# Attention pieces regrouped inside a dense FFN stream, with all queues in written order

## The chip, the cores and the metric

One core of one Trainium2 chip. The metric is the device time of one execution in microseconds (us), the median of several executions. "Span" is the time from the first to the last instruction in a profile; it is about 1.8 us shorter than the time of the same execution.

## The reference, cut to what matters

```python
# attention with K and V projected from 1024 rows to 64, then an FFN with a squared ReLU
k_proj = einsum('ks,bhsd->bhkd', E, k)        # q, k, v: 8 batches, 8 heads, 1024 rows, 64 columns
v_proj = einsum('ks,bhsd->bhkd', F, v)
attn   = softmax(q @ k_proj.T / 8)            # 1024 x 64 for each head
x      = (attn @ v_proj), heads side by side  # 8192 x 512
h      = maximum(x @ w_in, 0)                 # 512 -> 2048
out    = (h * h) @ w_out                      # 2048 -> 512
```

## The kernel before

The FFN of a batch is 62 steps in the order of TensorE's program. In batches 1 to 7 steps 0 to 15 and 31 to 46 are `x @ w_in` for half a batch (four matmuls of 512 columns each), and steps 16 to 30 and 47 to 61 are the second product, done as seven smaller products (in Strassen's manner) of 256-column matmuls. The attention of the next batch is cut into pieces, and tables say ahead of which step each goes:

```python
PIECES = {
    0: "transpose_q", 1: "copy_kp", 2: "copy_vp", 4: "copy_v_down",
    24: "scores 0, scores 1, exponentials 0", 25: "exponentials 1",
    27: "sums 0, values 0 0, reciprocals 0", 30: "values 0 1", 31: "normalize 0 0", 32: "normalize 0 1",
    47: "scores 2, scores 3, exponentials 2", 48: "exponentials 3",
    50: "sums 1, values 1 0, reciprocals 1", 53: "values 1 1", 54: "normalize 1 0", 55: "normalize 1 1",
}
```

A set of sums or values is eight matmuls side by side, each on 64 rows by 32 columns of TensorE's array (the eight start within 0.03 us). Their results go to a PSUM buffer (PSUM is the memory that TensorE writes to):

```python
def quads(self, g, weights):
    ps = att_psum([P, 2, TCH], F32)          # one of two PSUM buffers
    for a in range(2):
        for j in range(4):
            o, bank = PLACE[j % 2, a]
            nc.tensor.matmul(
                ps[32 * j:32 * j + 32, a, :], lhsT=weights(o, 4 * g + j),
                rhs=self.exp[2 * g + j // 2][o, bank, :], start=True, stop=True,
                tile_position=(o.start, 32 * j))
```

Q and the projected K are transposed by DMAs on SyncE's queue; Q, K and V are loaded, with a cast to bf16, by GpSimd's. There is one buffer each for Q, K, V and the transposed Q. The loop that places it all:

```python
with tc.manual_schedule(engines=ORDERED):    # TensorE, VectorE, ScalarE in written order
    ...
    for b in range(B):
        for n, g in enumerate(ffn_groups(b, cur.xT)):
            ...
            if nxt:
                for name, args in calls((BATCH_1, BATCH_2, PIECES)[min(b, 2)], n):
                    getattr(nxt, name)(*args)
                if n == (35, 12, 1)[min(b, 2)]:
                    ahead = load_batch(b + 2)
                if b and n == 53 and ahead:
                    ahead.project()
            g()
```

The softmax here doesn't subtract the row's maximum and nothing guards it: scores larger than these inputs give would overflow.

## Time and profile before

| | before |
|---|---|
| time, median | 487.8 us |
| span of the profile | 485.8 us |
| first FFN matmul | 19.90 us |
| batch 1 begins | 83.48 us |
| batch 1 / batches 2 to 5 / batch 6 / batch 7 | 60.26 / 57.61 / 55.89 / 55.8 us |

TensorE is busy 97% of the span, so the profile must be read for two small things: how long a batch is between the first FFN matmuls of two batches, and where a start comes later than the one before it explains. I call **cost in the stream** of a piece: the start of the first FFN matmul after it, less the start of the last one before it, less what that one takes alone (0.216 us with 512 columns, 0.109 with 256). The lines that carry the reading are in the prediction.

### The profile page before, as it was taken

The numbers are of one execution on the slowest core, as the hardware profiler recorded it, in microseconds if no ns is written. First come the engines' busy times: TensorE is split into PE (matmuls) and PEld (weight loads), VectorE is DVE, ScalarE is ACT, GpSimd is POOL, SyncE is SP. The second block draws the span as 40 slices with busy tenths as digits, with TensorE's granted clock in tenths as the row PEclk, the third lists the DMA queues.
The fourth block names the chain that finished last, engine by engine and source line by source line (L and its number), as shares of the span: only waits on it lengthen the run. The fifth ranks groups of instructions, "written<-read, shape, count | busy, mean of one in ns | idle before, by whom it ended". The sixth has DMA issues, their size and how long they took to land.

```text
span 485.8 us, 8378 instructions
## 1 busy us (share of the span) xinstructions
PE 472.6 (97%) x3614; PEld 292.3 (60%) x3614; DVE 315.4 (65%) x380; ACT 262.4 (54%) x414; POOL 33.2 (7%) x46
## 2 busy tenths in 40 slices
PE   4899999999999999999999999999999999999997
PEld 2444677475574845757475665747557474666656
DVE  2478855566848568495765848566694856848383
ACT  2487445665727556355655467264672746645351
POOL 6330020010020000100010000200000000000000
PEclk9999999999999999999999999999999999999999
DMA  9999999997389124991149921893232102020202
GB/s 162 204 205 206 164 144 219 235 170 178 46 145 226 30 88 86 172 187 44 44 89 194 162 88 20 141 220 66 88 74 68 45 0 88 2 88 0 88 0 88
DMA packets 72501, 55.46 MB, mean 114 GB/s; under 512 B 33936, under 2 KB 64656, under 8 KB 72464
## 3 DMA queue, kind: packets, MB, share of 16 engines
q0 software_dynamic: 30336, 29.36, 38.5%
q1 hardware_dynamic: 42128, 25.56, 20.7%
q8 instruction: 28, 0.46, 0.4%
q14 instruction: 9, 0.07, 0.0%
HBM read 59.24 MB, written 16.78 MB: 156 GB/s over the span
## 4 chain that ended last, share of the span: by engine, by line
PE 85%; DMA 10%; ACT 2%; POOL 1%; issue 1%; DVE 0%; POOLq 0%; DVEq 0%
PE ps_h L441 39%; PE ps_y L461 23%; PE ps_z L461 11%; DMA V_sb<-in_v_dram 7%; PE ps_x L461 5%; DMA w_in<-in_moe_w_in_dram 2%; PE ps_att L216 2%; PE ps_kv L175 2%; PE ps_att L201 2%; DMA kT<-kp 1%; ACT h_relu L492 1%; PE ps_kv L176 0%; POOL K_sb L91 0%; DVE hsq L500 0%; ACT hsq L498 0%
## 5 line engine op out<-in xcount | busy, mean ns | idle before, releaser
L441 PE MATMUL ps_h<-xT,w_in 128*128 128x512 bf16 x1024 | 225.0, 379 | 0.2 <-DMA w_in<-in_moe_w_in_dram 0.2
L500 DVE TENSOR_TENSOR hsq<-h_relu 128x1024 bf16<-128x1024 f32 x123 | 150.2, 1222 | 67.4 <-ACT h_relu L492 66.8
L492 ACT ACTIVATE h_relu<-ps_h 128x512 f32<-128x512 f32 x256 | 150.6, 597 | 66.2 <-PE ps_h L441 65.7
L441 PEld LDWEIGHTS <-w_in 128*128 128x128 bf16 x1024 | 99.5, 98 | 118.2 <-issue 1.8
L461 PEld LDWEIGHTS <-s 128*128 128x128 bf16 x1024 | 98.4, 98 | 19.6 <-issue 8.1
L461 PEld LDWEIGHTS <-hsq 128*128 128x128 bf16 x768 | 73.2, 98 | 19.4 <-issue 3.0
L461 PE MATMUL ps_y<-T,s 128*128 128x256 bf16 x512 | 62.4, 273 | 0.1
L574 DVE TENSOR_TENSOR o_sb<-ps_z,p_b 128x512 f32<-128x512 f32 x16 | 11.1, 692 | 52.9 <-issue 25.7
L455 DVE TENSOR_TENSOR s<-hsq 128x1024 bf16<-128x1024 bf16 x64 | 43.6, 684 | 0.0
L570 ACT COPY o_sb<-ps_y 128x512 f32<-128x512 f32 x15 | 8.8, 585 | 55.4 <-PE ps_y L461 55.4
L235 DVE TENSOR_TENSOR xT<-ps_att,rs 128x1024 bf16<-128x1024 f32 x28 | 33.0, 1217 | 7.3 <-ACT rs L229 7.3
L461 PE MATMUL ps_y<-w_out,hsq 128*128 128x256 bf16 x256 | 34.5, 273 | 0.3 <-DVE hsq L500 0.3
L461 PE MATMUL ps_x<-w_out,hsq 128*128 128x256 bf16 x256 | 33.2, 273 | 0.0
L461 PE MATMUL ps_y<-T,hsq 128*128 128x256 bf16 x256 | 31.7, 272 | 0.0
L208 ACT ACTIVATE expT<-ps_att 128x1024 bf16<-128x1024 f32 x28 | 27.4, 1028 | 6.4 <-PE ps_att L201 6.4
L461 PE MATMUL ps_z<-T,s 128*128 128x256 bf16 x256 | 30.8, 273 | 0.0
L461 PE MATMUL ps_z<-w_out,s 128*128 128x256 bf16 x256 | 30.6, 273 | 0.0
L570 ACT COPY p_b<-ps_y 128x512 f32<-128x512 f32 (+1 forms) x17 | 9.5, 560 | 28.1 <-PE ps_y L461 28.0
L78 POOL DMA_DIRECT2D Q_sb<-in_q_dram x7 | 6.1, 876 | 263.2 <-DMA qT<-Q_sb 262.8
L574 DVE TENSOR_TENSOR o_sb<-ps_y,p_d 128x512 f32<-128x512 f32 (+1 forms) x17 | 11.2, 660 | 19.2 <-PE ps_y L461 19.2
L228 ACT ACTIVATE rs<-ps_att 128x1024 f32<-128x1024 f32 x14 | 14.3, 1023 | 14.6 <-PE ps_att L216 14.6
L455 DVE TENSOR_TENSOR s<-s,hsq 128x1024 bf16<-128x1024 bf16 x32 | 21.9, 687 | 0.5
(74 smaller groups left out, 239.3 us busy)
## 6 DMA issues: line engine op xcount, KB each, us to landing
out_dram<-o_sb SPq DMA_DIRECT2D x30, 512.0 KB, 3.3
K_sb<-in_k_dram POOLq DMA_DIRECT2D x7, 1024.0 KB, 17.3
V_sb<-in_v_dram POOLq DMA_DIRECT2D x7, 1024.0 KB, 22.4
Q_sb<-in_q_dram POOLq DMA_DIRECT2D x7, 1024.0 KB, 9.6
w_in<-in_moe_w_in_dram POOLq DMA_DIRECT2D x8, 256.0 KB, 13.7
w_out<-in_moe_w_out_dram POOLq DMA_DIRECT2D x4, 512.0 KB, 13.2
K_sb<-in_k_dram POOLq DMA_DIRECT2D x2, 512.0 KB, 7.8
V_sb<-in_v_dram POOLq DMA_DIRECT2D x2, 512.0 KB, 12.7
```

What stands on the lines that cost most here:

```text
L175: nc.tensor.matmul(ps[0:KP, :], lhsT=ET[:, i, :], rhs=kv[:, :, i, :], start=f, stop=l)
L201: nc.tensor.matmul(ps[o, bank, :], lhsT=self.kT[r, 2 * pr + j, :], start=True, stop=True, rhs=self.qT[r, NT * (2 * pr + j):NT * (2 * pr + ...
L208: nc.scalar.activation(e[:], self.ps["s", pr][:], AF.Exp, scale=SCALE)
L228: nc.scalar.activation(rs[:], self.ps["r", g][:], AF.Ln)
L235: nc.vector.tensor_tensor(out=self.xT[:, 2 * g + e].rearrange("p a n t -> p a (n t)"), in0=self.ps["v", g, e][:], in1=self.rs[g][:], op=AL ...
L441: nc.tensor.matmul(ps[:], lhsT=w_in_blk(cb, fb), rhs=xT[:, cb, :, 2 * ch:2 * ch + 2], start=(cb == 0), stop=(cb == NCB - 1),)
L455: nc.vector.tensor_tensor(out=s[o][:, js], in0=x, in1=y, op=op)
L461: nc.tensor.matmul(ps[tb] if len(ps) == 2 else ps[0][:, tb], lhsT=lhs[:, j, tb * P:(tb + 1) * P], rhs=rhs[:, j], start=first and n == 0 an ...
L492: nc.scalar.activation(r[:, n], ps[:], AF.Relu)
L500: multiply = lambda: nc.vector.tensor_tensor(out=o, in0=r[:], in1=r[:], op=ALU.mult)
L570: nc.scalar.copy(to[:, t], ps)
L574: nc.vector.tensor_tensor(out=to[:, t], in0=ps, in1=more[:, t], op=ALU.add)
```

## The change

Its intent: fewer changes between FFN and attention on TensorE (five pieces a batch), pieces in batches 0 and 1 moved to where their data are there, and SyncE and GpSimd no longer ordered by the scheduler at build time but as written.

```diff
-ORDERED = {PE, DVE, Activation}
+ORDERED = {PE, DVE, Activation, Pool, SP}
     PIECES = {
-        0: "transpose_q", 1: "copy_kp", ...
-        24: "scores 0, scores 1, exponentials 0", 25: "exponentials 1",
-        27: "sums 0, values 0 0, reciprocals 0", 30: "values 0 1", ...
-        47: "scores 2, scores 3, exponentials 2", 48: "exponentials 3",
-        50: "sums 1, values 1 0, reciprocals 1", 53: "values 1 1", ...
+        1: "copy_kp", ...
+        20: "scores 0, scores 1, exponentials 0", 21: "exponentials 1",
+        23: "sums 0, values 0 0, reciprocals 0", 26: "normalize 0 0",
+        28: "scores 2, scores 3, exponentials 2", 29: "exponentials 3",
+        47: "values 0 1, sums 1, reciprocals 1", 48: "normalize 0 1",
+        53: "values 1 0, values 1 1", 54: "normalize 1 0", 55: "normalize 1 1",
     }
     BATCH_1 = {                                  # attention of batch 1, during batch 0
-        32: "project", 33: "copy_kp, transpose_q, copy_vp", ...
-        46: "scores 0, scores 1, ...", 49: "sums 0, values 0 0, ...", 52: "..., values 0 1", ...
-        54: "scores 2, scores 3, ...", 57: "sums 1, values 1 0, ...", 60: "values 1 1, normalize 1 1",
+        33: "project", 34: "copy_kp, transpose_q, copy_vp", ...
+        48: "scores 0, scores 1, ...", 51: "scores 2, scores 3, ...",
+        55: "sums 0, sums 1, logs 0, logs 1, inverses 0", 57: "inverses 1",
+        58: "values 0 0, values 0 1, ...", 61: "values 1 0, values 1 1, normalize 1 0",
     }
-    BATCH_2 = {**PIECES, ..., 9: "project", 10: "copy_kp", ...}
+    BATCH_2 = {12: "project", 13: "copy_kp, transpose_q", ..., 24: "scores 0, scores 1, ...",
+        27: "scores 2, scores 3, ...", 30: "sums 0, sums 1, logs 0", ...,
+        47: "values 0 0, values 0 1", 53: "values 1 0, values 1 1", ...}
     SECOND_HALF = {                              # second half of batch 0's own attention
-        9: "second_half 1 0, second_half 0 1",
+        9: "second_half 1 0", 10: "second_half 0 1",
-    ON_SCALAR = {(0, 1): (2, 4, 6), (1, 0): (4, 6)}
+    ON_SCALAR = {(0, 1): (2, 4, 6), (1, 0): (3, 5)}
-            elif b == 0:
+            elif b + ch == 1:                    # batch 1 too opens with x blocks 0 and 1 alone
+                    if b and n == 33 and ahead:
+                        ahead.transpose_q()
```

Cut: the split of the reciprocals into logs and inverses, one more square held back on VectorE in batch 0, three sums put off by two steps, the load order K, V, Q for batch 1, the start of batch 3's loads, and the last normalization of batch 1 after batch 0's last step.

## The prediction

> **What bounds the kernel now.** I read the page's engine row first, then the windows by batch, then what TensorE waited for, then the order of its work around the small attention matmuls, and last the queue of SyncE.
>
> The engine row of the page: TensorE (PE) is busy for nearly the whole span, VectorE and ScalarE are near two thirds.
>
> ```profile
> PE 472.6 (97%) x3614; PEld 292.3 (60%) x3614; DVE 315.4 (65%) x380; ACT 262.4 (54%) x414; POOL 33.2 (7%) x46
> ```
>
> The windows cut the span at the first FFN matmul of each batch (columns: stretch, length, then busy time of each engine). Start-up is the first 26 us, batch 0 ends at 83.48, batch 1 at 143.74.
>
> ```profile
> core 0: us, PE busy (x) PEld busy (x) DVE busy (x) ACT busy (x) POOL busy (x), PEclk, DMA share, GB/s
> 26.00:83.48 57.48, 56.19 (x488) 34.61 (x487) 41.08 (x55) 34.56 (x53) 6.74 (x8) 1.00 1.11 187
> 83.48:143.74 60.26, 60.00 (x450) 36.56 (x448) 38.37 (x46) 33.61 (x52) 5.26 (x6) 1.00 0.87 155
> 143.74:201.35 57.61, 57.61 (x435) 35.57 (x433) 38.81 (x45) 31.94 (x50) 2.63 (x3) 1.00 0.59 115
> 374.17:430.06 55.89, 55.81 (x419) 34.79 (x417) 37.93 (x43) 31.94 (x50) 0.00 (x0) 1.00 0.12 41
> ```
>
> Batches 2 to 5 take 57.61 us with TensorE busy in all of it. Batch 1 is longer mainly because two projections (of batches 2 and 3) fall into it; one takes 1.85 us (133.95 to 135.80 in the order of time). Only batches 0 and 1 have idle gaps. The list of TensorE's waits is short, and its first line belongs to the start, which the change leaves alone:
>
> ```profile
> PE ps_E L138 <- DVE e_bf L134: 5.6, 1, 5.6
> PE ps_att L201 <- DMA kT<-kp: 0.5, 1, 0.5
> PE ps_att L286 <- DMA Q_sb<-in_q_dram: 0.4, 1, 0.4
> PE ps_y L461 <- DVE hsq L500: 0.3, 1, 0.3
> PE ps_kv L176 <- DMA V_sb<-in_v_dram: 0.2, 1, 0.2
> ```
>
> The order of time in a settled batch shows what an attention piece costs inside the FFN stream (start, duration, what; only starts are used):
>
> ```profile
> 166.08 1.04 PE L461 MATMUL ps_y<-T,s 128*128 128x256 bf16 x8
> 167.04 0.41 PE L216 MATMUL ps_att<-expT,ones 64*32 64x512 bf16 x8
> 167.27 0.40 PE L216 MATMUL ps_att<-expT,vp 64*32 64x512 bf16 x8
> 167.60 1.05 PE L461 MATMUL ps_y<-T,s 128*128 128x256 bf16 x8
> 168.48 1.04 PE L461 MATMUL ps_x<-w_out,hsq 128*128 128x256 bf16 x8
> 169.43 1.03 PE L461 MATMUL ps_y<-T,hsq 128*128 128x256 bf16 x8
> 170.39 0.41 PE L216 MATMUL ps_att<-expT,vp 64*32 64x512 bf16 x8
> 170.74 1.05 PE L461 MATMUL ps_y<-T,hsq 128*128 128x256 bf16 x8
> ```
>
> Eight FFN matmuls run start to start in 0.88 us undisturbed (167.60 to 168.48), but in 0.96 us when a piece follows (166.08 to 167.04, 169.43 to 170.39). A piece of one set of eight costs 0.35 + 0.09 = 0.44 us, a piece of two sets 0.56 + 0.09 = 0.65 us. Two single sets joined into one piece so save 2 x 0.44 - 0.65 = 0.23 us.
>
> SyncE's queue around the second and third batch (start, time to issue):
>
> ```profile
> 57.73 5.02 SPq L167 DMA_TRANSPOSE qT<-Q_sb  x1
> 62.81 1.25 SPq L185 DMA_TRANSPOSE kT<-kp  x1
> 66.36 0.43 SPq L625 DMA_DIRECT2D out_dram<-o_sb  x1
> 79.29 12.77 SPq L167 DMA_TRANSPOSE qT<-Q_sb  x1
> 94.48 1.22 SPq L185 DMA_TRANSPOSE kT<-kp  x1
> ```
>
> The transpose of Q at 79.29 meets the loads of batch 2's K and V and takes 12.77 us to issue; the settled ones take 4.7.
>
> **What the Trainium skill says.** "TensorE: Matmul & The Clock Gate", section "Back-to-back issue gap", gives N/2.4 + 2.5 ns between matmuls on a warm clock: 216 ns for 512 columns, 109 for 256. The trace agrees: in the chain of work 64 FFN matmuls of 512 columns take 13.81 us (216 ns), 16 of 256 columns 1.75 us (109 ns), at a granted clock of 1.00. So what is left to gain is in the pieces and the waits, not in the FFN. "TensorEngine Tiling (Array Packing)", section "Key Properties", says that changing the tiling mode drains TensorE; the 0.09 us ahead of every piece, where 128x128 changes to 64x32, fits. "DMA: Bandwidth & Descriptors", section "Issuing engines are not separate DMA queues", says that DMAs of all issuing engines end on the same 16 and interleave; the 12.77 against 4.7 us above agrees. The same trace's transposes of Q land 6.7 us after issue at best, 7.3 in the median, 16.4 at worst.
>
> **The change part by part.** One FFN batch has 62 steps: 16 of four 512-column matmuls (0.863 us each) and 15 of mostly eight 256-column ones (0.873 us) for each half; in batch 0 both halves' first products come first.
>
> Fewer pieces. In PIECES, the third batch's table and the second's, six pieces a batch (scores, sums with values, values, twice) become five (scores, scores and three of two sets each). No matmul is added or removed. 7 batches x 0.23 = 1.6 us, all on TensorE's path, as TensorE has no slack.
>
> First half-batch. The transposes of Q's second half move one step later (9 to 10). They waited 0.40 us for Q, whose load landed at 29.7; a step is 0.86 us, so the 0.40 goes. A square is held back behind the copy of the transposes; VectorE has gaps there (0.8 and 1.3 us), so no cost.
>
> Second batch. Its projection moves from step 32 to 33. It started at 52.03 and its V landed at 52.63; it ended at 54.49, 2.46 us for 1.9. One step later, V is there: 0.56 saved. The transpose of K is now ahead of that of Q in SyncE's queue. K's copies end near 56, Q's load lands at 57.64, so Q is issued about as before and lands near 66.3, as before. The scores came at step 46 and waited until 66.72. They now come two steps (1.75 us) later, near 67.3, and the 0.5 us wait goes.
>
> Opening of batch 1. The last two x blocks come late by design: values 1 0 and 1 1 at step 61 and the last normalization after it, while the FFN opens with eight matmuls on blocks 0 and 1 (1.73 us). ScalarE: the four reciprocal activations (1.02 to 1.06 each) start at step 55 behind a copy, so the first reciprocal is ready 3.8 us after that step begins and the first normalization ends near 5.1. VectorE then does normalization (1.2), two adds (0.65 each) and the last two normalizations in a row. By this count values 1 1 waits some 0.2 us for its PSUM buffer (two, freed by the normalizations), and block 3 is ready 0.4 us before it is wanted. Cost +0.2.
>
> Third batch. The projection moves from step 9 to 12; V(2) landed at 91.48 and step 12 is near 92.4, so no wait. Q's transpose moves behind K's at step 13, after the loads. From the start of batch 1: 12 steps 10.4, projection 1.9 = 12.3; VectorE first finishes a sum that waits for ScalarE's square, then K's two copies, 13.9; K's issue 1.25, so Q is issued at 15.1 and lands 6.7 to 7.3 later: 21.8 to 22.4. The scores at step 24 come at 13.8 + 1.9 + 6.1 = 21.8. Cost 0 to 0.6, say +0.3. The 0.3 us wait for the last square in batch 1 should go with the squares moved to ScalarE at 3 and 5 and three sums put off: -0.26.
>
> Settled batches. Q's transpose moves to step 33 of the batch before; K's stays, now behind the last store, about 1.5 us later. K's landing took 10.5 us in the median, so near 12.5 after the batch's start; scores at step 20 come at 16.4. No wait, no gain.
>
> Sum: -1.6 - 0.40 - 0.56 - 0.5 - 0.26 + 0.2 + 0.3 = -2.8. From 487.81: 485.0 us.
>
> **Rivals.** First, a wait moves instead of going: Q(2)'s transpose lands late. If it met loads it would take 16.4 us and TensorE would lose about 9 us, 494. Against it: the loads of batch 3 stand behind Q's buffer, which is freed only when this transpose lands (GpSimd's waits on it total 262.8 us), so it runs nearly alone. A loss of 1 us is possible, giving 486.
>
> Second, given order blocks SyncE or GpSimd: a store waiting for VectorE holds a transpose behind it. SyncE waits 238 us in total for such adds, so blocking is real, but each transpose behind a store has slack of 4 us or more in the settled batches. If K landed 2 us after it is wanted in four batches, 493. GpSimd's order was already the written one at the start, so nothing is lost there.
>
> Third, the opening of batch 1 stalls by 1 to 2 us because the normalizations pile up: 486 to 487.
>
> Fourth, the waits go but what they hid appears behind them, so that only the pieces count: 486.2.
>
> **Range and chances.** The gains are small and mostly arithmetic of the pieces; the losses have the longer tail, so the range is 484.0 to 487.0 around 485.0. Faster by 2% needs 478.1: that is 6.9 us more than I find, and TensorE has no idle time to give it after the start: 0.01. Slower needs 497.6, several rivals at once: 0.015. Within 2%: 0.975.
>
> **What would show it.** Right: batches 2 to 5 near 57.4 us with five pieces; batch 0 shorter by about 1.5; no TensorE wait for Q's load, for V at the second projection, for K's transpose. Wrong: a TensorE wait for a transpose at batch 1's scores above 0.6 us; a wait for VectorE's x at 82 to 86 us; settled batches at 57.6, which would mean that joined pieces save nothing; waits of TensorE that repeat in every batch, which would mean that the queue order bites.

## The result, and the profile after

The changed kernel took 485.42 us in the median of four executions (483.81 to 485.61), the kernel before 487.83 beside it. The ratio is 0.9938, 95% interval 0.9911 to 0.9965. The median lies in the prediction's range, 485.0 in 484.0 to 487.0.

The profiled execution was the fastest of the four, 483.81 us, with a span of 482.0. The engine row of the page after, and of TensorE's six waits the longest and the last two of the list:

```profile
PE 470.4 (98%) x3614; PEld 293.1 (61%) x3614; DVE 313.2 (65%) x380; ACT 261.8 (54%) x414; POOL 33.2 (7%) x46
```

```profile
PE ps_E L141 <- DVE e_bf L137: 5.6, 1, 5.6
...
PE ps_h L459 <- DVE xT L350: 0.4, 1, 0.4
PE ps_att L319 <- ACT expT L313: 0.2, 1, 0.2
```

All of these lie before 20.1 us. The waits for Q's load, for V, for K's transpose and for VectorE's square are gone. The windows by batch (same columns as in the prediction; batch 0 from 26 us, batch 1, batch 2, batch 6):

```profile
26.00:81.56 55.56, 55.44 (x490) 34.89 (x488) 40.13 (x54) 34.04 (x54) 6.67 (x8) 1.00 1.11 193
81.56:141.16 59.60, 59.52 (x451) 36.39 (x449) 38.79 (x47) 32.60 (x52) 5.27 (x6) 1.00 0.91 157
141.16:198.54 57.38, 57.38 (x434) 35.60 (x432) 38.54 (x45) 32.13 (x50) 2.63 (x3) 1.00 0.70 133
370.69:426.23 55.54, 55.54 (x419) 34.81 (x417) 37.67 (x43) 32.13 (x50) 0.00 (x0) 1.00 0.12 41
```

Against before, the start of batch 1 came 1.92 us earlier, batch 1 is 0.66 shorter, each of batches 2 to 5 is 0.23 shorter, and batch 6 0.35. This is the 3.8 us by which the spans differ. A joined piece in a settled batch (order of time on TensorE: start, duration, what):

```profile
183.17 0.41 PE L219 MATMUL ps_att<-expT,vp 64*32 64x512 bf16 x8
183.39 0.40 PE L219 MATMUL ps_att<-expT,ones 64*32 64x512 bf16 x8
183.73 1.05 PE L479 MATMUL ps_y<-w_out,hsq 128*128 128x256 bf16 x8
```

Two sets cost 0.56 us from start to FFN, as two sets did before, while a set alone took 0.35. SyncE's queue in batches 0 and 1, in written order:

```profile
56.60 1.30 SPq L188 DMA_TRANSPOSE kT<-kp  x1
58.02 4.83 SPq L170 DMA_TRANSPOSE qT<-Q_sb  x1
...
95.03 1.20 SPq L188 DMA_TRANSPOSE kT<-kp  x1
96.41 4.83 SPq L170 DMA_TRANSPOSE qT<-Q_sb  x1
```

K's transpose is ahead of Q's, and Q of batch 2 issues in 4.83 us, not 12.77: it no longer meets the loads of that batch. It landed at 103.06 us, and the scores that need it began at 103.53. The meeting has moved to the next batch: Q of batch 3, issued at 113.45 us beside the loads of K and V, took 17.64 us to issue and landed at 133.31; it is wanted only at 157.68.

One gain is in none of the lists. The second scores of batch 0 in the kernel before, and the FFN matmul after them:

```profile
74.61 0.84 PE L201 MATMUL ps_att<-qT,kT 64*64 64x512 bf16 x8
75.38 1.05 PE L461 MATMUL ps_y<-T,s 128*128 128x256 bf16 x8
```

The same two in the changed kernel:

```profile
69.29 0.63 PE L204 MATMUL ps_att<-qT,kT 64*64 64x512 bf16 x8
69.84 1.92 PE L479 MATMUL ps_z<-T,s 128*128 128x256 bf16 x16
```

0.77 against 0.55 us from start to start, for the same eight matmuls. The wait was inside the piece: the second four matmuls began at 75.04 us, just after VectorE's normalization of the values before them ended (74.99), which frees their PSUM buffer. No list of waits shows it, because the modelled ends of the first four (75.01) cover all but 0.02 us of it.

**The open question of the result.** The profile shows 3.8 us of gain, the medians 2.4. The other three executions had spans of 483.6 to 483.8 us. The experiments are about this as much as about the parts of the change.

### The profile page after: what moved, and what is told of

Its sections match the earlier page's. It is cut to its first block, busy times and chain, and to the rows that moved or that the text cites. A ratio compares the mean times of both kernels' runs of the same rounds, so it can differ in the third digit from the quotient of the medians.

```text
span 482.0 us, 8383 instructions
## 1 busy us (share of the span) xinstructions
PE 470.4 (98%) x3614; PEld 293.1 (61%) x3614; DVE 313.2 (65%) x380; ACT 261.8 (54%) x414; POOL 33.2 (7%) x46
## 4 chain that ended last, share of the span: by engine, by line
PE 93%; DVE 3%; ACT 2%; DMA 1%; issue 0%; SPq 0%
PE ps_h L459 44%; PE ps_y L479 23%; PE ps_z L479 11%; PE ps_x L479 6%; PE ps_kv L178 3%; PE ps_att L219 2%; PE ps_att L204 2%; DVE hsq L518 1%; DMA e_f<-in_F_dram 1%; PE ps_k L260 1%; DVE s L473 1%; DVE xT L244 0%; ACT expT L313 0%; DVE xT L350 0%; ACT h_relu L510 0%; PE ps_fill L360 0%
## 5 line engine op out<-in xcount | busy, mean ns | idle before, releaser
L479 PE MATMUL ps_y<-w_out,hsq 128*128 128x256 bf16 x256 | 33.2, 273 | 0.0
L473 DVE TENSOR_TENSOR s<-hsq,s 128x1024 bf16<-128x1024 bf16 x32 | 21.8, 684 | 0.0
L591 ACT COPY p_a<-ps_y 128x512 f32<-128x512 f32 (+1 forms) x17 | 9.4, 561 | 21.8 <-PE ps_y L479 21.6
## 6 DMA issues: line engine op xcount, KB each, us to landing
V_sb<-in_v_dram POOLq DMA_DIRECT2D x7, 1024.0 KB, 22.4
```

The source lines that it names most:

```text
L473: nc.vector.tensor_tensor(out=s[o][:, js], in0=x, in1=y, op=op)
L479: nc.tensor.matmul(ps[tb] if len(ps) == 2 else ps[0][:, tb], lhsT=lhs[:, j, tb * P:(tb + 1) * P], rhs=rhs[:, j], start=first and n == 0 an ...
L591: nc.scalar.copy(to[:, t], ps)
```

## The experiments

Twelve runs, in three groups. Each group ran on one chip with its own runs of the kernel before; times are compared through these.

### The changed kernel again, unaltered

> The changed kernel unaltered, to see the spread of its executions. Its profiled execution had a span of 482.0 us, the three timed ones 483.6 to 483.8. Theory A (a load with little slack): in the longer executions TensorE waits about 1.6 us at one of the two projections in batch 1, because V of batch 2 (landed 0.9 us before it was wanted in the profiled execution) or of batch 3 (1.6 us before) comes late; the profile then shows a wait for V at a projection whenever its own execution is long. Theory B (start-up): the whole run is shifted by 1.6 us before the first FFN matmul and batches 1 to 7 are equally long in all executions. Time 483.8 to 485.7 under both, median near 485.4.

484.44 us in the median (484.02 to 484.65), ratio 0.9927 (0.9915 to 0.9939). Its first FFN matmul came at 20.74 us, 0.73 later than in the first trace. From there on it is the same program in time: batch 0 61.48 us after 61.55, batch 1 59.60, batches 2 to 5 57.38. No wait for V anywhere. So theory A falls in this trace, and B holds: the difference lies before the first FFN matmul. (With a span of 482.6 us this was not one of the long executions; the trace with seven pieces below has a start as late as theirs would be, 21.93 us, and its batch 0 takes 61.47.)

### The kernel before again, unaltered

> The kernel before, unaltered, for a second trace of it. Theory (the spread of the times is start-up, which hangs on when TensorE's matmuls reach full rate): batches 1 to 7 have the same lengths as in its first trace (60.26, four of 57.6, 55.89, 55.8) within 0.05 us, and the whole difference of the spans lies before the first FFN matmul; ratio 1.000. Rival: the waits for loads in batches 0 and 1 move and the batches differ.

487.81 us, ratio 0.9993 (0.9981 to 1.0006). Batches 60.20, four of 57.6, 55.90, 55.8. The trace adds something that I had not expected. The first FFN matmul came at 19.75 us, 0.15 earlier than in the first trace, and yet batch 1 began at 83.48 us in both: batch 0 was 63.73 us long in place of 63.58. The kernel before is pinned there by something that does not move with its start: K's transpose for batch 1 landed at 66.68 us in the first trace and at 66.67 in this one, 16.8 us before batch 1 in both. So the rival, waits that move, holds for batch 0. Batches 1 to 7 kept their lengths within 0.06 us, where 0.05 was forecast.

### A late start on purpose, in both kernels

```diff
             self.copy_v(1)
             self.half_normalize(0, 0, 1)
+            filler(6)
```

> The kernel before with six dummy matmuls (1.3 us) just ahead of its first FFN matmul, a start that is late on purpose. Theory of absorption: the kernel before stands at three loads and transposes in batch 0 (0.48 us for Q, 0.55 for V, 0.58 for K's transpose, by their cost in the stream), which come when the load stream brings them; a late start shortens these waits, so batch 1 still starts at 83.4 to 83.7 us and the time is that of the kernel before within 0.3 us. Rival (the waits have nothing to do with it): +1.0 to +1.3 us.

> The changed kernel with the same six dummy matmuls. Theory of absorption: its batch 0 waits for no load any more, so the late start comes through: batch 1 starts 61.5 us after the first FFN matmul, and the time is 1.0 to 1.3 us above that of the changed kernel (484.4 on the second chip): 485.4 to 485.7. Rival: it absorbs as much as the kernel before, within 0.3 us of 484.4.

Kernel before: 488.25 us, ratio 1.0006 (0.9992 to 1.0019). Changed kernel: 485.51 us, ratio 0.9948 (0.9935 to 0.9962), which is 1.0 us above the changed kernel's 0.9927 by the ratios (0.0021 x 487.8). In the profiled executions the first FFN matmul came at 22.68 and 22.58 us, later than the six matmuls explain, because the start itself was slow. Batch 0 from its first FFN matmul, the kernel before with the late start, then the changed one:

```profile
22.68:84.54 61.86, 61.67 (x530) 36.92 (x529) 43.84 (x59) 37.12 (x58) 8.92 (x11) 1.00 1.11 185
```

```profile
22.58:84.06 61.48, 61.33 (x530) 36.91 (x529) 42.89 (x58) 36.56 (x58) 8.91 (x11) 1.00 1.08 185
```

Started 2.8 us late, the kernel before needs 61.86 us for batch 0 in place of 63.58: it takes 1.7 us back. In its list of TensorE's waits the three for loads and transposes in batch 0 are gone. The changed kernel takes 61.48, as from 20.74. So the waits in the kernel before were waits for a load stream that does not follow its start. A late start used them up; in the changed kernel there is nothing left to use up from a start of 20.7 us on, and a late start goes through to the end.

The stream is not quite fixed. In the late execution of the kernel before it was itself 1.0 us later (V of batch 1 landed at 53.64 us, 52.63 in the first trace; K's transpose at 67.73), and batch 1 again began 16.81 us after K's transpose: at 84.54 us, not at the forecast 83.4 to 83.7. Its batch 1 was 0.37 us longer than in the first trace, as the projection of batch 2 waited for V (2.38 us in the stream in place of 2.00). With starts of 19.9 and 20.0 the spans differ by 3.8 us (485.84 and 482.01), with 22.7 and 22.6 by 2.8 (487.26 and 484.48). The theory of absorption stands in both kernels and its rivals fall, with a blemish: the median of the kernel before rose by 0.4 us where at most 0.3 was forecast.

### Settled batches with seven pieces

```diff
-        47: "values 0 1, sums 1, reciprocals 1", 48: "normalize 0 1",
-        53: "values 1 0, values 1 1", ...
+        47: "values 0 1", 48: "sums 1, reciprocals 1, normalize 0 1",
+        52: "values 1 0", 53: "values 1 1", ...
```

> In the settled batches the two joined pieces (values 0 1 with sums 1, values 1 0 with values 1 1) are taken apart again: seven pieces in place of five, no work added. Theory of the pieces: 0.23 us for each piece, so batches 2 to 5 at 57.38 + 0.46 = 57.84 us and the kernel +2.3 us over five batches. Rival (the settled batches got shorter for another reason, such as the order of the queues or of VectorE's work): batches stay at 57.38 to 57.5.

486.84 us (486.34 to 487.88), ratio 0.9979: 2.4 us above the changed kernel of the same group. Batch 2 by the windows:

```profile
143.00:200.84 57.84, 57.84 (x434) 35.66 (x432) 38.52 (x45) 32.01 (x50) 2.63 (x3) 1.00 0.70 130
```

57.84 to the digit: two pieces more, 0.46 us more, no work more. The theory of the pieces stands.

This execution also shows where a late start is made. The second projection of K's half in the start-up, and what follows it, in the first trace of the kernel before and in this one:

```profile
11.27 1.06 PE L251 MATMUL ps_k<-K_sb,ET 128*64 128x256 bf16 x8
12.26 0.60 PE L351 MATMUL ps_fill<-ET 128*128 128x512 bf16 x2
```

```profile
12.16 1.91 PE L260 MATMUL ps_k<-K_sb,ET 128*64 128x256 bf16 x8
14.01 1.03 PE L360 MATMUL ps_fill<-ET 128*128 128x512 bf16 x2
```

Eight matmuls of 256 columns take 0.99 us start to start in the one and 1.85 in the other: TensorE had come to full rate in the first case and ran at about half in the second. (The column of the granted clock reads 1.00 in both stretches; only the durations tell.) Here full rate came only during the transposes of Q, between 15.7 and 17.6 us, and the first FFN matmul at 21.93. Of the 2.03 us by which that is later than in the kernel before, 0.7 were lost earlier, in the wait for F (1.17 us in place of 0.48). "TensorE: Matmul & The Clock Gate", section "What's actually happening", says that the clock gate opens after a window of activity which is free-running and does not begin with the kernel; that full rate came anywhere between about 10 and 17 us in these traces of the same instructions agrees.

### Dummy matmuls ahead of the start

```diff
     def E_and_F():
+        ps_warm = ffn_psum("ps_warm")
+        for _ in range(9):                       # on a constant tile, result unused
+            nc.tensor.matmul(ps_warm[:], lhsT=warm[:, 0:P], rhs=warm[:], start=True, stop=True)
```

> The changed kernel with nine dummy matmuls of 128x512 on TensorE ahead of everything, in the time in which it waits for E (to 5.6 us). Theory (the start-up spread is the moment at which TensorE comes to full rate): the full rate is there before the first products of K, the first FFN matmul comes at 19.9 to 20.1 us in every execution, where V and the weights limit it, and the times draw together at 483.7 to 484.1. Rival (the spread comes from the loads): the first FFN matmul stays between 20.0 and 21.9 us and the times between 483.8 and 485.7.

484.22 us (484.06 to 485.01), ratio 0.9925 (0.9913 to 0.9937): no better than the changed kernel's 0.9927. The trace shows why half of the theory fails. Full rate was there early: the first eight K matmuls took 0.99 us (8.12 to 9.11). The first FFN matmul came at 19.98, as expected. But on the way there TensorE waited for K's load (0.7 us) and V's (0.5), and after it for weights (0.13 and 0.24 us) and for V of batch 1 (the projection cost 2.10 us in the stream, 1.94 without a wait): batch 0 was 62.05 us long, 0.5 over the changed kernel's. So an early start meets the load stream in the changed kernel too (two experiments below that leave its batch 0 alone agree: begun at 19.79 us it took 61.87, the projection at step 33 costing 2.30, and begun at 20.56 it took 61.74, the projection costing 2.19, with V 0.8 us later than in the first trace); it earns the half microsecond by which the first FFN matmul was late in other executions and gives it back. In the kernel of the next paragraph the same dummies did not even hold the rate: there the first eight K matmuls took 1.84 us (8.69 to 10.53). The times did not draw together either (484.06 to 485.01). A miss, and not a way to a steady start.

### Two small waits taken out

```diff
-        28: "scores 2, scores 3, exponentials 2", 29: "exponentials 3",      # PIECES
+        29: "scores 2, scores 3, exponentials 2", 30: "exponentials 3",
-        53: "values 1 0, values 1 1", 54: "normalize 1 0", 55: "normalize 1 1",   # BATCH_2
+        54: "values 1 0, values 1 1", 55: "normalize 1 0", 56: "normalize 1 1",
-                    if b and n == 53 and ahead:
+                    if b and n == (53 if b > 1 else 54) and ahead:
```

> Two small waits of the changed kernel taken out: in the settled batches the second scores come at step 29 in place of 28 (0.08 us each, five batches), and in batch 1 the last values and the projection come at step 54 in place of 53 (values 1 1 waited 0.27 us there for a PSUM buffer that VectorE's normalization frees). Theory: batches 2 to 5 at 57.30 us, batch 1 at 59.33, in all -0.6 to -0.7 us after the first FFN matmul. Rival: the waits move to the next step, nothing gained.

483.56 us (483.41 to 484.55), ratio 0.9911 (0.9898 to 0.9925). Batch 1 by the windows:

```profile
82.01:141.34 59.33, 59.33 (x450) 36.27 (x448) 38.80 (x47) 32.60 (x52) 5.27 (x6) 1.00 0.89 158
```

59.33 after 59.60, and batches 2 to 5 57.31 or 57.30 after 57.38: both to the digit. The two waits were found by the cost in the stream, not in the list: the second scores of a settled batch cost 0.73 us where scores otherwise cost 0.65, and the piece with the projection in batch 1 2.77 where the same in batch 2 costs 2.50.

Both together, with the dummies:

> Both of the former together: if both theories hold the gains add, 483.1 to 483.5 us; if the dummy matmuls do nothing, 483.3 to 485 with the spread of the changed kernel.

483.47 us (483.13 to 483.81), ratio 0.9903 (0.9888 to 0.9918). It falls in the range for added gains, but its start was late (20.76 us, as told above), so the gain is that of the two moves; the intervals of the two kernels overlap. From the first FFN matmul to the end the two take 461.24 and 461.28 us, the changed kernel 461.91 and 462.00. By the times both beat the kernel before; that they beat the changed kernel rests on the traces, since the interval of the first overlaps that of the changed kernel, which ran on another chip.

### Batch 1's opening not by pieces of x

```diff
-            elif b + ch == 1:
+            elif b == 0:
```

> Batch 1's FFN opens whole again (each step's four matmuls over all x blocks) and not by pieces of x. The last x block of batch 1 is ready 1.5 us after TensorE starts the batch in the changed kernel (83.1 against 81.6) and would be wanted 0.65 us after the start. Theory: TensorE waits 0.8 to 1.0 us for VectorE there, and nothing else changes: +0.9 us. Rival: the slack elsewhere (the scores of batch 1, the projection) hides it, or the opening itself cost a bank wait: within 0.3.

485.12 us, ratio 0.9940, 0.7 us above the changed kernel of the group. Batch 1 was 60.53 us, 0.93 longer, and the list of waits names it:

```profile
PE ps_h L459 <- DVE xT L244: 0.8, 1, 0.8
```

So the late last blocks of x, which the table of the second batch brings with it, would cost 0.9 us, and the opening by pieces pays for them.

### The two queues ordered by the scheduler

```diff
-    mybir.EngineType.PE, mybir.EngineType.DVE, mybir.EngineType.Activation, mybir.EngineType.Pool,
-    mybir.EngineType.SP,
+    mybir.EngineType.PE, mybir.EngineType.DVE, mybir.EngineType.Activation,
```

> Given order for TensorE, VectorE and ScalarE alone, as before; SyncE and GpSimd are ordered by the scheduler at build time. Theory of the pieces and positions: the order of the two queues is worth nothing by itself, within 0.5 us of the changed kernel, unless the scheduler puts the transpose of Q of batch 2 back among the loads; then V of batch 2 or the scores of batch 1 come late and TensorE waits 1 us or more there. Rival (the given order is what gained): most of the 2.4 us is lost again, batches 2 to 5 above 57.5.

486.43 us (484.99 to 487.53), ratio 0.9968 (0.9952 to 0.9984), 2.0 us above the changed kernel of the group. The scheduler did put Q of batch 2 among the loads again (SyncE's queue), and TensorE waited in batch 1, but for K's transpose:

```profile
77.47 12.75 SPq L169 DMA_TRANSPOSE qT<-Q_sb  x1
```

```profile
PE ps_att L203 <- DMA kT<-kp: 0.7, 1, 0.7
```

Q landed at 92.33 us, well in time. Its buffer was then free early, so batch 3's loads began at 92.88 us (103.62 in the changed kernel). K's transpose, issued at 95.49 beside them, landed 9.2 us later, in place of 2.6. Batch 1 is 60.35 us, 0.75 longer; batches 2 to 5 stay at 57.38. So the order is worth nothing in the settled batches and something in batch 1. The profiled execution was the fastest of six (spans 483.2 to 485.8), so what the others lost beyond 0.75 us is not shown.

### Two positions in batch 0 put back

```diff
-        33: "project", 34: "copy_kp, transpose_q, copy_vp", 37: "copy_v_down",
+        32: "project", 33: "copy_kp, transpose_q, copy_vp", 36: "copy_v_down",
-        9: "second_half 1 0", 10: "second_half 0 1",
+        9: "second_half 1 0, second_half 0 1",
```

> The changed kernel with two of its positions in batch 0 put back: the transposes of Q's second half at step 9, and the second batch's projection at step 32. Theory: with a start at 20.0 us TensorE again waits for Q's load (0.48 us) and for V at the projection (0.55 us), so batch 0 is up to 1.0 us longer; where the start is later by d, the waits shorten by d, so batch 1 starts at 82.6 to 83.0 us whatever the start. Rival (the gain in batch 0 came from the merged pieces and the scores two steps later alone): batch 0 stays at 61.5 us after the first FFN matmul.

484.94 us (484.63 to 485.09), ratio 0.9937. The first FFN matmul came at 21.07 us, 1.1 late, and batch 1 at 82.75, inside the forecast 82.6 to 83.0. Q's wait was all but gone (cost in the stream 0.90 us for scores and transposes, which is 0.44 + 0.45), and the projection cost 2.16 us, 0.22 over one without a wait (1.94). With this start the two positions are worth 0.2 us (batch 0 61.68 against 61.48), not 1.0. That agrees with absorption; an early start of this kernel was not seen, so the 1.0 us rests on the kernel before.

### The third batch projected at step 9

```diff
-        12: "project", 13: "copy_kp, transpose_q", 14: "copy_vp", 17: "copy_v_down",
+        9: "project", 10: "copy_kp, transpose_q", 11: "copy_vp", 14: "copy_v_down",
```

> The changed kernel with the third batch projected at step 9 of batch 1, as before, not at 12. V of batch 2 lands at 91.1 us, and step 9 comes near 89.4 to 90.1. Theory: TensorE waits 1.0 to 1.8 us for V there, less of it where the start was late; the square at the end of batch 1's first half, on ScalarE at 3 and 5, may wait too; +1 to +2 us in batch 1 (60.6 to 61.4 us). Rival: the projection's position is neutral, batch 1 stays at 59.6.

488.95 us (487.71 to 491.21), ratio 1.0022 (1.0004 to 1.0041): 4.6 us above the changed kernel by the ratios (1.0022 - 0.9927 = 0.0095, times 487.8). Batch 1 was 63.42 us, 3.8 longer, more than forecast. Its waits:

```profile
PE ps_y L479 <- DVE hsq L518: 1.4, 1, 1.4
...
PE ps_kv L179 <- DMA V_sb<-in_v_dram: 0.8, 1, 0.8
```

V is what I forecast (the projection cost 3.15 us in the stream, 1.2 over the changed kernel's 1.94). The rest, 2.6 us, is mostly three further waits: for ScalarE's copy of V, for its ReLU and for VectorE's last square. My reading is that the squares which ScalarE takes (3 and 5) are fitted to a projection at step 12, and that with it at 9 they collide with the copies; a run with the projection at 9 and the old squares (4 and 6), which would show it, was not made.

## Why the prediction was right, point by point

The sum of the prediction was -2.8 us. The traces, start-up left out, give -3.96: the first FFN matmul to the end takes 465.94 us before (485.84 - 19.90) and 462.00 after (482.01 - 20.01), and 461.91 in the second trace. The medians give -2.4 and, by the second group's ratio, -3.6. The number was right with two errors that worked against each other: the gain after the start was 1.1 us larger than forecast, and a part of it does not reach the median. That 485.0 came so near to 485.42 is partly luck.

- **Fewer pieces.** Predicted 0.23 us each in seven batches. Measured 0.23 in batches 2 to 5 (57.61 to 57.38, where two small things cancel: the second scores cost 0.73 us in place of 0.65, and a hitch of 0.07 between two FFN matmuls is gone), 0.22 in batch 0 by the pieces' cost, 0.35 in batch 6, where a single set had cost 0.59 and not 0.44. In batch 1 nothing came of it, since the joined last values waited 0.27 us for a PSUM buffer (the second set began at 131.03 us, the normalization that frees it ended at 130.98); moving them one step gave exactly that back. Seven pieces gave +0.46. The mechanism and the size hold.
- **First half-batch.** Predicted 0.40; by cost in the stream 0.48 (1.36 to 0.44 + 0.45).
- **Second batch.** The projection: 0.56 predicted, 0.55 measured (2.55 to 2.01). The first scores: 0.5 predicted, 0.58 measured (1.23 to 0.65). Missed: the second scores, 0.22, a wait that is in no list.
- **Opening of batch 1.** +0.2 predicted for values 1 1, nothing came: the second normalization ended at 80.2 us, just before they needed its buffer. The last block was ready before it was wanted. The margins were right to some tenths; the experiment with the whole opening shows 0.9 us at stake.
- **Third batch.** Q's transpose was predicted at 15.1 us after the batch's start and landed 21.8 to 22.4 after it; it was issued at 14.85 and landed at 21.5, with the scores at 22.0 (21.8 predicted). So +0.3 became 0. The wait for the last square: -0.26 predicted, -0.53 by cost in the stream (0.43 and 0.10 in the kernel before, nothing after).
- **Settled batches, queue order.** K's transpose landed 13.4 us after the start of batch 2 (12.5 predicted), wanted at 16.5. No wait, as said. The rival that given order blocks a queue falls; in the trial with free queues it was K's transpose of batch 2 that came late, beside loads which Q's early transpose had let in. Not foreseen: Q of batch 3, at its new place in step 33, meets the loads (19.9 us to landing), with 24 us to spare.

The mis-sized terms add up to the difference between 2.8 and 4.0: 0.08 (Q) + 0.08 (first scores) + 0.22 (second scores) + 0.2 (opening) + 0.3 (third batch) + 0.27 (square), less 0.17 (pieces 1.44 in place of 1.6, and the projection's 0.01), and 0.16 of small things around batch 1, among them a hitch of 0.09 at its opening in the kernel before. That is 1.14.

What the prediction did not have at all is that the waits of batch 0 are not a fixed amount. It took 0.40, 0.56 and 0.5 us as losses that every execution has. They are the distance between a start that varies and a load stream that does not follow it: two traces of the kernel before begin batch 1 at 83.48 us with different starts, and with a start 2.8 us late batch 1 begins only 1.06 later, as much as the stream was late. In a late execution these waits are small already, so removing them gains less. This would explain why the medians gained less than the trace with the early start. That the other timed executions of the first group began late is inferred from their spans and from the equal lengths of batches 1 to 7 in all traces of the kernel; these executions have no trace.

## What to carry to other kernels

Where one engine is full, count its cost from start to start across each change of work; a list of waits leaves out what hides inside a piece, and the two moves that took a further 0.6 to 0.7 us off this kernel's traces were found so. Before you add up waits for loads at the front of a kernel as gains, ask whether they move with the start: a wait for a stream with its own pace absorbs jitter of the start, and a kernel without it is faster and passes that jitter on. This is read from the traces; the spread of the times does not show it (0.6 and 1.8 us in two groups of the changed kernel, 0.8 to 1.7 in the groups of the one before). A position in a table may hang together with the division of work between two engines around it: here the projection put back alone cost 3.8 us in its batch.

## What the Trainium skill lacked or had wrong

- "TensorE: Matmul & The Clock Gate", section "Back-to-back issue gap", gives some 131 ns for each 512-column matmul as the sustained rate with weight loads between, and calls the 216 ns of its formula too high there. Here every matmul has its own weight load, and 64 in a row take 13.81 us, 216 ns each: the formula holds, the 131 ns do not.
- "TensorEngine Tiling (Array Packing)", section "Key Properties", says that a change of tiling mode drains TensorE, without a size. Here 0.09 us ahead of each piece, and 0.22 to 0.23 us saved for each two pieces joined.
- "TensorE: Matmul & The Clock Gate", section "HAM oscillation — how this bites in real kernels", has as its rule that TensorE should have no idle gaps over about 3.4 us (the page goes on to a fall after frequent short idles, in another setting and with no size of them). In the kernel with the dummies and the two moves the rate fell with no gap over 1.0 us once the dummies had begun: two fill matmuls at 7.32 us took 0.61 us (1.03 at half rate in the first trace), and the K matmuls from 8.69 on took 1.84 for eight (0.99 at full rate).
- "DMA: Bandwidth & Descriptors", section "DMA Transpose (X-bar)", gives no duration for a transpose, alone or among loads (the page has a bandwidth for it elsewhere). Here the transpose of Q for one batch landed 6.7 us after issue (96.41 to 103.06) with no load under way, and that of the next batch after 19.9 us (113.45 to 133.31) beside the loads of K and V.
